# High parts of a square copied in SBUF, and subtractions issued a step later, in an attention-and-channel-mix kernel

## The chip, the cores and the metric

The kernel runs on one core of one Trainium2 chip. Five engines work beside each other, each from a queue of its own and in that queue's order: TensorE (PE, with its weight loads shown as PEld) multiplies matrices into PSUM, VectorE (DVE) and ScalarE (ACT) work on PSUM and SBUF, GpSimd (POOL) works on SBUF, and SyncE (SP) issues DMAs. The metric is the device time of one execution in microseconds.

## The reference

Four batches of 12,608 tokens of 128 channels go through an attention over 32 inducing points and then through a channel mix:

```python
h = mab(I, x)
return mab(x, h).astype(np.float32)          # attn_out, B x N x 128
...
xk = mu_k * x + (1.0 - mu_k) * x_prev
xr = mu_r * x + (1.0 - mu_r) * x_prev
k = np.maximum(xk @ w_k, 0.0)
v = k * k @ w_v
r = 1.0 / (1.0 + np.exp(-(xr @ w_r)))
return (r * v).astype(np.float32)
```

`mab(q, kv)` is softmax attention with kv as keys and values; `x_prev` is `x` moved by one token. The hidden width of the channel mix is 1,024.

## The kernel before

The channel mix is cut into groups of 512 tokens (25 in a batch, the last of 320) and each group into four units of two chunks of the hidden width: 400 units, numbered `n`. For one unit, `up` (L800) multiplies into a PSUM buffer `ps_a`, of which there are two; `square` (L803 to L819) makes the squared ReLU; `down` (L829) multiplies it with `w_v` into `ps_v`. The products run on operands of type fp32r, so that a factor is split in two: a high part `kh`, rounded to fp32r, and a low part `kl`, which is the square less `kh`. `down` takes three products: high with high, high with the low weights, and low with high.

In `square`, VectorE takes the ReLU from PSUM into `k` (L810). The high part is then the square of `k` on ScalarE (L815), or, for the units in the set `high_vector`, the product of the ReLU of `ps_a` and `k` on VectorE (L812), which reads PSUM once more. ScalarE squares `k` in place (L816), and GpSimd subtracts, `kl = k - kh` (L818). `k` has four buffers, `kh` five and `kl` four.

The order of all instructions is written out by hand in the loop at L1011. In step `n` it issues, if `n` is even, the up products of units `n` and `n + 1`; then the work listed in `early`; then `square` of unit `n` with its subtraction; then the gate product `zgate` (once in a group), `store`, `down` of unit `n - 4`, and last what is listed in `events` for this step. `gate` (L834) of a finished group stands at the head of a step.

`events` holds the preparation of what comes later. While the units of one batch run, in stretches of twelve steps, each of six stretches has `stage_a` of the following batch (its scores against the inducing points, L340 to L452) and `stage_b` (the second attention of the next block of the same batch, L617 to L663, with DMAs that lay out its results as `R`). `combine` closes the sum of a batch at its end. The last batch has no following one, so that its stretches hold only `stage_b`. `high_vector` is filled in the same loop (L993): with `s` the first step of a stretch, units `s + 4` and `s + 8`, 48 in all; each batch has some 28 units behind its six stretches in which none is on VectorE.

At the start, `head` and `start` run the first batch's attention and the conversion of the weights. Their last parts stand in `events` of steps 0 and 1: `place(3)` in step 0 holds L115, the conversion L109 on GpSimd and L110 on ScalarE, and L120; `place` in step 1 holds L123, L127, L133 on GpSimd, and `split_wv` with L162 on ScalarE and L163 on GpSimd. Aside from these and its share of the weights before, GpSimd's queue holds nothing but the 400 subtractions.

Of the kernel before, what the change touches and what calls it, by code (L numbers as in the profile page):

```python
# [8 lines left out]
F32 = mybir.dt.float32  # L9
# [4 lines left out]
ALU = mybir.AluOpType  # L14
# [5 lines left out]
def kernel(  # L20
# [11 lines left out]
    nc = tc.nc  # L32
# [741 lines left out]
    class Group:  # L774
# [28 lines left out]
        def square(self, u, on_vector):  # L803

            w = self.w
            k = mp.tile([P, UC * G], F32, name="k_t", bufs=4).rearrange("p (c t) -> p c t", c=UC)[:, :, :w]
            kh = mp.tile([P, UC, G], F32R, name="kh", bufs=5)[:, :, :w]
            kl = mp.tile([P, UC, G], F32R, name="kl", bufs=4)[:, :, :w]
            ps = self.ps.pop(u)[:, :, :w]
            nc.vector.tensor_scalar(out=k, in0=ps, scalar1=0.0, scalar2=None, op0=ALU.max)  # L810
            if on_vector:
                nc.vector.scalar_tensor_tensor(out=kh, in0=ps, scalar=0.0, in1=k,  # L812
                                               op0=ALU.max, op1=ALU.mult)
            else:
                nc.scalar.activation(out=kh, in_=k, func=AF.Square)  # L815
            nc.scalar.activation(out=k, in_=k, func=AF.Square)  # L816
            self.h[u] = (kh, kl)
            return lambda eng, a, z: eng.tensor_tensor(out=kl[:, :, a:z], in0=k[:, :, a:z],  # L818
                                                       in1=kh.bitcast(F32)[:, :, a:z], op=ALU.subtract)  # L819

        def down(self, u):
            w = self.w
# [33 lines left out]
    def run(th):  # L856
        for f in th:
            f()
# [51 lines left out]
    def head():  # L910


        last = NBLK - 1
        for k in range(2):
            ab[k].tr()
        ab[0].scores()
        for k in range(NBLK):
            ab[k].maxi()
            ab[k].expo()
            if k > 0:  # L920
                ab[k - 1].hmm()
                ab[k - 1].acc()
            if k == last:
                maxes()
            if k == 0:
                constants()
            if k + 2 < NBLK:
                ab[k + 2].tr()
            place(PARTS[k][1])
            if k == last:  # L930
                ab[k].sums()
                weights()
            ab[k].etrans()
            ab[k].ecopy()
            if k < last:
                ab[k].sums()
                ab[k + 1].scores()
        weights_sum()
        place(2)
        ab[last].hmm()  # L940
        ab[last].acc()
        load_x(1, 0)
        place(1)
        hfin()
        place(1)
# [11 lines left out]
    def start():  # L957

        def bank():
            return pv.tile([P, G], F32, name="ps_v")  # L960

        wk = wpart(0, bank)
        wg = wpart(1, bank)
        sc0, df0, ex0, nm0, hi0, lo0, turn0, put0, idle = stage_b_first(0)
        sc1, df1, ex1, nm1, hi1, lo1, turn1, put1, _ = stage_b_first(1)
        run([sc0, wk[0], sc1, df0, ex0, nm0, wk[1], hi0, wk[2], lambda: idle(2), lambda: turn0(0), lambda: put0(0),
             lo0, lambda: turn0(1), lambda: put0(1)])
        run([df1, ex1])
        at(0, lambda: place(3))
        at(1, lambda: place(len(work)))  # L970
        at(0, wg[0])
        (b_scores, b_trans, b_maxi, b_sub, b_expo, b_total, b_recip, b_mult, b_back, b_high, b_low,
         b_spread) = stage_b(0, 0, None, 0, "a")
        for f in (nm1, hi1):
            soon(1, f)
        for n, fs in ((0, (b_scores,)), (2, (b_trans, b_maxi, b_sub, b_expo)),
                      (3, (b_total, b_recip, b_mult, b_back, b_high)), (4, (b_low,))):
            for f in fs:
                at(n, f)
        for i in range(2, Q):  # L980
            at(i + 3, lambda i=i: b_spread(i))
            at(i + 5, lambda i=i: double(batches[0], i))
        for n, f in ((1, lo1), (1, wg[1]), (1, wg[2]), (2, lambda: turn1(0)), (2, lambda: turn1(1)),
                     (2, lambda: put1(0)), (2, lambda: put1(1)), (2, lambda: units[0][0].zgate())):
            at(n, f)

    SEG = 12
    high_vector = set()
    for b in range(B):
        t = b * UB + (4 if b == 0 else 0)  # L990
        for j in range(NBLK - 1):
            s = t + SEG * j
            high_vector |= {s + 4, s + 8}  # L993
            if b + 1 < B:
                stage_a(b + 1, j, at, s)
            stage_b(b, j + 1, at, (s - 2 if j == (b == 0) else s + 1) if b or j else 4, direct=b == j == 0)
        if b + 1 < B:
            s = t + SEG * (NBLK - 1)
            combine(b + 1, at, s)
            stage_b(b + 1, 0, at, s + 10)  # L1000
    units = []
    for b in range(B):
        for g in range(NG):
            grp = Group(b, g)
            units += [(grp, u) for u in range(NU)]
    end = len(units) - 1
    late = []
    with tc.manual_schedule():
        head()
        start()  # L1010
        for n in range(len(units) + LAG + 2):  # L1011
            grp, u = units[n] if n < len(units) else (None, n % NU)
            old, ou = units[n - LAG] if LAG <= n < len(units) + LAG else (None, 0)
            m = n - LAG - 1
            if 0 <= m < len(units) and units[m][1] == NU - 1:
                units[m][0].gate()
            if grp is None:
                run(late)
                late = []
            else:  # L1020
                if n % 2 == 0:
                    for g, v in units[n:n + 2]:
                        g.up(v)
                run(early.pop(n, []))
                low = grp.square(u, n in high_vector)
                run(late)
                late = []
                part = grp.w - (grp.w // 2 if n >= len(units) - 3 else 0)
                low(nc.gpsimd, 0, part)
                if part < grp.w:  # L1030
                    late = [lambda low=low, a=part, z=grp.w: low(nc.vector, a, z)]
                if n == end:
                    run(late)
                    late = []
                if n >= NU and u == 1:
                    grp.zgate()
            if 1 <= m <= len(units) and units[m - 1][1] == NU - 1:
                units[m - 1][0].store()
            if old is not None:
                old.down(ou)  # L1040
            run(events.pop(n, []))
# [30 lines left out]
```

## Time and profile before

| what | us |
|---|---|
| median of 3 runs | 1134.17 |
| lowest and highest | 1133.51, 1136.06 |
| the profiled execution | 1133.0 |
| its span, first to last instruction | 1131.1 |
| TensorE busy | 1074.4 |
| VectorE busy | 912.4 |
| ScalarE busy | 963.7 |
| GpSimd busy | 955.0 |

The page's shares (95%, 81%, 85% and 84% of the span in the order of the table) are averages. Matmuls are pipelined and their busy time counts waits within the pipeline, so that a TensorE that is busy throughout need not be at its peak. The mean granted TensorE clock was 0.978 of full speed; it was below 0.9 only in the first 113 us. In the profile, a row of a group gives line, engine, operation, target and sources, shapes, count, then busy time and mean nanoseconds of one, then the idle time of the engine ahead of it and what ended it. A row of the timeline gives start and length in microseconds, and in square brackets the idle time ahead and what ended it.

### The profile page before, as it was taken

What the parts mean: (1) busy time and instruction counts of PE and PEld (TensorE: products, weight loads), DVE (VectorE), ACT (ScalarE), POOL (GpSimd) and SP (SyncE); (2) the same over time, 40 slices, a digit from 0 to 9 for tenths busy, and PEclk for the clock granted to TensorE, in tenths of its full rate; (3) what the DMA queues carried; (4) which work ended last, traced back from release to release, by engine and by line L of the source; (5) the groups of instructions that cost most, each with busy time, mean ns of one, the idle gap of its engine ahead of it and who ended that gap; (6) DMA issues with size and microseconds to landing.
All of it is one profiled execution on the core that took longest, in us unless ns stands there. A gap on an engine that the chain in (4) does not pass through costs nothing.

```text
span 1131.1 us, 19193 instructions
## 1 busy us (share of the span) xinstructions
PE 1074.4 (95%) x6530; PEld 735.9 (65%) x6530; DVE 912.4 (81%) x1289; ACT 963.7 (85%) x1103; POOL 955.0 (84%) x422
## 2 busy tenths in 40 slices
PE   7647999999999999999999999999999999999996
PEld 5424666666766666666767666666667666667775
DVE  3666889998787899998677899998777788888665
ACT  5356788998898989899998989989899989999994
POOL 1245788889888998889889898889889889999996
PEclk9768999999999999999999999999999999999999
DMA  9204476677216746766416656766424425443422
GB/s 265 82 3 110 94 156 143 159 165 167 50 28 139 166 115 150 171 146 142 85 25 127 144 123 154 159 134 146 79 44 94 76 50 105 85 94 75 88 37 34
DMA packets 268209, 124.64 MB, mean 110 GB/s; under 512 B 225904, under 2 KB 247440, under 8 KB 265808
## 3 DMA queue, kind: packets, MB, share of 16 engines
q1 hardware_dynamic: 267776, 123.40, 51.0%
q8 instruction: 52, 0.85, 0.3%
q14 instruction: 45, 0.37, 0.1%
q10 hardware_dynamic: 336, 0.02, 0.0%
HBM read 28.07 MB, written 25.82 MB: 48 GB/s over the span
## 4 chain that ended last, share of the span: by engine, by line
PE 77%; DVE 6%; POOL 5%; issue 4%; SPq 3%; ACT 3%; DMA 2%; DVEq 0%; ACTq 0%; POOLq 0%
PE ps_v L829 44%; PE ps_a L800 24%; POOL kl L818 4%; PE ps_v L788 3%; DVE k_t L810 2%; PE pb_b L617 2%; PE pb_a L368 2%; PE pb_a L437 1%; SPq L343 1%; SPq L192 1%; DMA kl<-in_x_dram 1%; ACT k_t L816 1%; ACT kh L815 1%; DMA R<-hl 1%; SPq L597 1%
## 5 line engine op out<-in xcount | busy, mean ns | idle before, releaser
L818 POOL TENSOR_TENSOR kl<-k_t,kh 128x1024 fp32r<-128x1024 f32 (+2 forms) x400 | 936.1, 2372 | 128.4 <-ACT k_t L816 103.3
L810 DVE TENSOR_SCALAR k_t<-ps_a 128x1024 f32<-128x1024 f32 (+1 forms) x400 | 477.2, 1198 | 94.6 <-PE ps_a L800 67.8
L816 ACT ACTIVATE k_t<-k_t 128x1024 f32<-128x1024 f32 (+1 forms) x400 | 417.8, 1047 | 51.7 <-DVE kh L812 18.9
L815 ACT ACTIVATE kh<-k_t 128x1024 fp32r<-128x1024 f32 (+1 forms) x352 | 365.1, 1037 | 63.7 <-DVE k_t L810 62.5
L800 PE MATMUL ps_a<-R,W 64*128 64x512 f32 (+1 forms) x2400 | 333.9, 408 | 18.1 <-DVE k_t L810 7.0
L800 PEld LDWEIGHTS ps_a<-R,W 64*128 64x128 f32 x2400 | 210.5, 186 | 140.4 <-issue 57.1
L829 PE MATMUL ps_v<-kh,wvh 128*128 128x512 f32 (+1 forms) x800 | 271.7, 421 | 0.0
L829 PE MATMUL ps_v<-kl,wvh 128*128 128x512 f32 (+1 forms) x800 | 247.3, 390 | 2.2 <-POOL kl L818 1.2
L829 PE MATMUL ps_v<-kh,wvl 128*128 128x512 f32 (+1 forms) x800 | 246.6, 390 | 0.0
L829 PEld LDWEIGHTS ps_v<-kh,wvh 128*128 128x128 f32 x800 | 132.8, 189 | 94.6 <-issue 35.1
L829 PEld LDWEIGHTS ps_v<-kl,wvh 128*128 128x128 f32 x800 | 149.7, 188 | 35.5 <-POOL kl L818 2.7
L829 PEld LDWEIGHTS ps_v<-kh,wvl 128*128 128x128 f32 x800 | 149.7, 188 | 33.4
L834 DVE TENSOR_TENSOR oT<-ps_v,rT 128x512 f32<-128x512 f32 (+1 forms) x100 | 66.9, 669 | 22.7 <-PE ps_v L829 22.0
L845 DVE STREAM_TRANSPOSE ot<-oT 128x512 f32<-128x512 f32 x96 | 67.0, 698 | 0.0
L788 PE MATMUL ps_v<-R,Wg 128*128 128x512 f32 (+1 forms) x200 | 63.1, 397 | 0.6 <-DVE oT L834 0.5
L812 DVE SCALAR_TENSOR_TENSOR kh<-ps_a,k_t 128x1024 fp32r<-128x1024 f32 x48 | 58.8, 1225 | 1.7
L790 ACT ACTIVATE rT<-ps_v 128x512 f32<-128x512 f32 (+1 forms) x100 | 57.8, 578 | 0.3
L340 DVE STREAM_TRANSPOSE xs<-xb 128x512 f32<-128x512 f32 x72 | 49.9, 694 | 3.6 <-DMA R<-hl 1.9
L788 PEld LDWEIGHTS ps_v<-R,Wg 128*128 128x128 f32 x200 | 36.6, 189 | 11.5 <-DVE oT L834 3.0
L790 ACT ACT_TABLE_LOAD x31 | 39.8, 1283 | 0.5
L663 DVE TENSOR_TENSOR hl<-pb_b,hl 128x512 fp32r<-128x512 f32 x23 | 15.8, 689 | 14.8 <-ACT hl L660 14.5
L617 PE MATMUL pb_b<-xt,hT 128*32 128x512 f32 x184 | 24.4, 603 | 0.0
(212 smaller groups left out, 538.4 us busy)
## 6 DMA issues: line engine op xcount, KB each, us to landing
out_dram<-ot SPq DMA_DIRECT2D x184, 128.0 KB, 3.3
R<-R SPq DMA_DIRECT2D x90, 256.0 KB, 3.3
xb<-in_x_dram SPq DMA_DIRECT2D x18, 1024.0 KB, 5.9
xt<-xs SPq DMA_DIRECT2D x288, 64.0 KB, 2.0
R<-hl SPq DMA_DIRECT2D x98, 128.0 KB, 2.4
R<-hl SPq DMA_DIRECT2D x98, 127.8 KB, 2.4
kh<-in_x_dram SPq DMA_DIRECT2D x4, 512.0 KB, 8.2
kl<-in_x_dram SPq DMA_DIRECT2D x4, 512.0 KB, 7.6
```

Of the source, the lines that this page charges most:

```text
L340: nc.vector.transpose(out=xs.rearrange("p (s q) -> p s q", q=M), in_=S.xb[j][:, :, M * c:M * (c + 1)])
L788: nc.tensor.matmul(out=ps[:, :w], lhsT=S.Wg, rhs=R[:, s, :w], start=(s == 0), stop=(s == 1))
L790: nc.scalar.activation(out=self.rT, in_=ps[:, :w], func=AF.Sigmoid)
L800: nc.tensor.matmul(out=ps[:, r, :w], lhsT=S.W[a][rows, u * P:(u + 1) * P], rhs=R[rows, k, :w], start=(n == 0), stop=(n == 2))
L810: nc.vector.tensor_scalar(out=k, in0=ps, scalar1=0.0, scalar2=None, op0=ALU.max)
L812: nc.vector.scalar_tensor_tensor(out=kh, in0=ps, scalar=0.0, in1=k, op0=ALU.max, op1=ALU.mult)
L815: nc.scalar.activation(out=kh, in_=k, func=AF.Square)
L816: nc.scalar.activation(out=k, in_=k, func=AF.Square)
L818: return lambda eng, a, z: eng.tensor_tensor(out=kl[:, :, a:z], in0=k[:, :, a:z], in1=kh.bitcast(F32)[:, :, a:z], op=ALU.subtract)
L829: nc.tensor.matmul(out=self.v, lhsT=wt[:, fc, :], rhs=kk[:, c, :], start=(fc == 0 and n == 0), stop=(fc == FC - 1 and n == 2))
L834: nc.vector.tensor_tensor(out=self.oT, in0=self.v, in1=self.rT, op=ALU.mult)
L845: nc.vector.transpose(out=ot[:, o:o + w], in_=self.oT)
```

## The change

`square` now returns two functions. `high` copies the finished square `k` from SBUF into `kh` on VectorE, for the units of `high_vector`; for these units ScalarE does only the square in place. `low` is the subtraction on GpSimd. Both are issued in the following step, behind that step's `square`; only the last four units keep them in their own step, with the tail's halves as before. Four units in twelve are in `high_vector` in place of two.

```diff
-            if on_vector:
-                nc.vector.scalar_tensor_tensor(out=kh, in0=ps, scalar=0.0, in1=k,
-                                               op0=ALU.max, op1=ALU.mult)
-            else:
+            if not on_vector:
                 nc.scalar.activation(out=kh, in_=k, func=AF.Square)
             nc.scalar.activation(out=k, in_=k, func=AF.Square)
             self.h[u] = (kh, kl)
-            return lambda eng, a, z: eng.tensor_tensor(out=kl[:, :, a:z], in0=k[:, :, a:z],
-                                                       in1=kh.bitcast(F32)[:, :, a:z], op=ALU.subtract)
+
+            def low(eng, a, z):
+                eng.tensor_tensor(out=kl[:, :, a:z], in0=k[:, :, a:z],
+                                  in1=kh.bitcast(F32)[:, :, a:z], op=ALU.subtract)
+
+            def high():
+                if on_vector:
+                    nc.vector.tensor_copy(out=kh, in_=k)
+            return high, low
...
-            high_vector |= {s + 4, s + 8}
+            high_vector |= {s + 1, s + 4, s + 8, s + 10}
...
-                low = grp.square(u, n in high_vector)
-                run(late)
-                late = []
+                high, low = grp.square(u, n in high_vector)
+                run(late + after)
+                late, after = [], []
                 part = grp.w - (grp.w // 2 if n >= len(units) - 3 else 0)
-                low(nc.gpsimd, 0, part)
+                if n < len(units) - 4:
+                    after = [high, lambda low=low, z=grp.w: low(nc.gpsimd, 0, z)]
+                else:
+                    high()
+                    low(nc.gpsimd, 0, part)
```

More of the change, by code (lines that the diff above doesn't have):

```diff
@@ L1024 @@
                 run(early.pop(n, []))
-                low = grp.square(u, n in high_vector)
-                run(late)
-                late = []
+                high, low = grp.square(u, n in high_vector)
+                run(late + after)
+                late, after = [], []
                 part = grp.w - (grp.w // 2 if n >= len(units) - 3 else 0)
-                low(nc.gpsimd, 0, part)
+                if n < len(units) - 4:
[3 more added lines that the diff above has]
+                    low(nc.gpsimd, 0, part)
                 if part < grp.w:
```

## The prediction

> **What bounds the kernel now.** I read the windows view first, cut into stretches of twelve units, because the page's shares average over stages with different limits. Its columns are the length of the stretch, then busy microseconds (and instructions) of each engine.
>
> ```profile
> core 0: us, PE busy (x) PEld busy (x) DVE busy (x) ACT busy (x) POOL busy (x), PEclk, DMA share, GB/s
> ...
> 686.98:718.88 31.90, 31.90 (x201) 21.53 (x199) 29.84 (x43) 28.66 (x33) 28.71 (x13) 1.00 0.63 142
> ...
> 916.71:946.35 29.64, 29.64 (x160) 20.61 (x158) 25.13 (x30) 27.11 (x29) 26.39 (x12) 1.00 0.42 80
> 946.35:976.00 29.65, 29.65 (x161) 20.62 (x159) 25.14 (x30) 27.54 (x31) 28.48 (x13) 1.00 0.44 81
> 976.00:1005.64 29.64, 29.64 (x160) 20.61 (x158) 25.12 (x30) 27.35 (x30) 28.43 (x13) 1.00 0.41 81
> 1005.64:1034.60 28.96, 28.96 (x160) 20.62 (x159) 24.38 (x30) 26.76 (x29) 27.77 (x13) 1.00 0.45 84
> 1034.60:1063.24 28.64, 28.64 (x153) 20.47 (x151) 22.00 (x27) 27.21 (x31) 28.64 (x13) 1.00 0.42 82
> ```
>
> In the middle of a batch (first row) TensorE is never idle and sets the 31.90 us; VectorE is left 2.06 us and GpSimd 3.19 us. In the last batch no following batch is prepared, TensorE has less to do, and the stretch falls to 29.65 and then 28.64 us, where GpSimd is busy throughout: twelve subtractions are then the bound. Next I read the page's groups for the edited lines.
>
> ```profile
> L818 POOL TENSOR_TENSOR kl<-k_t,kh 128x1024 fp32r<-128x1024 f32 (+2 forms) x400 | 936.1, 2372 | 128.4 <-ACT k_t L816 103.3
> ...
> L815 ACT ACTIVATE kh<-k_t 128x1024 fp32r<-128x1024 f32 (+1 forms) x352 | 365.1, 1037 | 63.7 <-DVE k_t L810 62.5
> ...
> L845 DVE STREAM_TRANSPOSE ot<-oT 128x512 f32<-128x512 f32 x96 | 67.0, 698 | 0.0
> ...
> L812 DVE SCALAR_TENSOR_TENSOR kh<-ps_a,k_t 128x1024 fp32r<-128x1024 f32 x48 | 58.8, 1225 | 1.7
> ```
>
> **What the edits remove and add.** High parts on VectorE go from 2 to 4 in twelve, 48 to 96. ScalarE loses 48 squares of 1.037 us, 49.8 us over the run, 2.07 us a stretch. That is worth little by itself: in the middle TensorE is full, and ScalarE was not its limit. VectorE loses 2 x 1.225 us a stretch and gains four copies.
>
> No copy from SBUF to SBUF of this size is in the trace. The nearest row is a one-input operation between SBUF tiles, 512 elements wide.
>
> ```profile
> L115 DVE TENSOR_SCALAR xs<-k_t x4: 415/420/421, 20.9 to 62.7; 128x512 int32<-128x512 int32 x4
> ```
>
> It took 0.420 us, where the transpose of 512 elements (L845) took 0.698. The 0.278 us between them is what 256 elements cost L845, 1.09 ns each, so L115 handled elements two at a time. 1,024 elements in pairs should take what 512 take singly, **0.69 us**. The other end is singly, 1.22 us, as L812. I take 0.69, since L115 is the same kind of operation; open is whether an fp32r target keeps the pace. The Trainium skill, VectorE: DVE Perf Modes, section The perf-mode tier table, gives fp32 copies in SBUF twice the pace of operations with two inputs; the L115 row agrees for int32, and no row shows it for fp32r.
>
> VectorE per middle stretch: 29.84 - 2.45 + 4 x 0.69 = 30.15 of 31.90 us, if no copy has to wait. But there are rows that say it will.
>
> ```profile
> 310.77 2.41 POOL L818 TENSOR_TENSOR kl<-k_t,kh 128x1024 fp32r<-128x1024 f32 x1 [1.61 <-ACT k_t L816]
> ...
> 312.29 0.93 DVE L524 TENSOR_SCALAR mk<-stack,rd 128x32 f32<-128x32 f32 x1
> ```
>
> ```profile
> 65.01 2.37 POOL L818 TENSOR_TENSOR kl<-k_t,kh 128x1024 fp32r<-128x1024 f32 x1 [11.78 <-ACT k_t L816]
> ```
>
> ```profile
> 65.71 2.21 DVE L123 SCALAR_TENSOR_TENSOR e1t<-k_t,e1t 128x512 f32<-128x512 uint32 x1
> ```
>
> ```profile
> L123 DVE SCALAR_TENSOR_TENSOR e1t<-k_t,e1t x4: 681/688/2210, 25.7 to 65.7; 128x512 f32<-128x512 uint32 x4
> ```
>
> ```profile
> 1114.24 5.58 POOL L818 TENSOR_TENSOR kl<-k_t,kh 128x1024 fp32r<-128x1024 f32 x4
> ```
>
> ```profile
> 1115.30 4.87 DVE L818 TENSOR_TENSOR kl<-k_t,kh 128x320 fp32r<-128x320 f32 x1
> ```
>
> L524, a one-input operation of 32 elements from SBUF, began inside a GpSimd subtraction and ended at 313.22, just behind that subtraction's end (313.18). L123 (median 0.688 us) took 2.21 us and ended 0.54 us behind GpSimd's end at 67.38. The narrow L818 on VectorE started at 1115.30 and ended at 1120.17, 0.35 us behind the last of four subtractions in a row (1119.82). So these VectorE operations wait for GpSimd, and the third got no turn between two subtractions. The Trainium skill, SBUF — State Buffer, section Who interferes with whom, has this as an exclusive lock on a port pair, held for a whole instruction, and counts copies in pairs under it. These three rows agree with the blocking; by a page without that rule the copies would cost nothing beyond 30.15 us, which is the second rival below.
>
> ```profile
> 63.88 1.06 ACT L816 ACTIVATE k_t<-k_t 128x1024 f32<-128x1024 f32 x1
> ```
>
> ```profile
> 697.85 9.53 POOL L818 TENSOR_TENSOR kl<-k_t,kh 128x1024 fp32r<-128x1024 f32 x4 [1.61 <-PE ps_a L800]
> ```
>
> What a copy then does: it stands in VectorE's queue behind the next unit's ReLU, and behind it stand that step's other VectorE work and the following ReLU, for which TensorE waits. The subtraction of the same unit waits for the copy, and the copy waits for the subtraction before it. So GpSimd stands still once per copied unit, at least 0.55 us (L123's rest for 512 elements) plus 0.07 us to start again (65.01, behind ScalarE's end at 64.94) and 0.03 us of lost overlap (a subtraction of 2.41 us follows the last by 9.53 / 4 = 2.38): with rounding, **0.66 us**, 0.80 (0.69 + 0.11) if the copy shares nothing with the wait, more if VectorE comes late.
>
> **Last batch.** Four copies cost GpSimd 4 x 0.66 = 2.6 us on twelve subtractions of 2.38 (28.5 us): 31.1 us. Against 29.64, 29.65, 29.64, 28.96 and 28.64 that is 1.5 x 3 + 2.1 + 2.5 = **+9** us. At 0.80 it is +12; if TensorE's lead on the entering side absorbs part, +5.
>
> **Middle stretches.** GpSimd at 31.1 of 31.90 still fits, so the price is what VectorE's waiting does to TensorE.
>
> ```profile
> 684.40 1.22 DVE L810 TENSOR_SCALAR k_t<-ps_a 128x1024 f32<-128x1024 f32 x1
> ```
>
> ```profile
> 685.38 1.67 PE L800 MATMUL ps_a<-R,W 64*128 64x512 f32 x12
> ```
>
> ```profile
> 700.13 1.22 DVE L810 TENSOR_SCALAR k_t<-ps_a 128x1024 f32<-128x1024 f32 x1
> ```
>
> The ReLU that ends at 685.62 frees the PSUM buffer for the second half of the up product of 685.38 (from 686.2, half of 1.67 us later): 0.6 us to spare. The copy of unit s+1 now comes ahead of it, 0.69 us, so 0.1 us is missing with no wait at all. Behind the ReLU of 700.13, which ends at 701.35, stands the copy of s+8; GpSimd's row of four from 697.85 gives it a turn at 702.6 (two of 2.38), so VectorE stands 1.3 us and copies until 703.2. L812 of the same unit, 1.23 us, is gone ahead of it, but the copies of s+4 and s+10 wait likewise. VectorE has 1.75 us a stretch to spare and four copies with waits of some 0 to 1.3 us: about 2.6 us, an overdraft of **0.8 us** a stretch (0 to 2.4, when each waits a whole 1.04 us). Twelve full stretches (four in each of three batches) at 0.8 and three lighter ones at 0.3: **+10.5** us (0 to 30).
>
> **Batch changes.** The chain of waits runs through the edited lines there.
>
> ```profile
> 617.39 1.07 ACT kh L815
> ...
> 624.81 1.23 DVE kh L812
> ...
> 626.18 0.98 PE ps_a L800 x6
> ```
>
> The square at 617.39 belongs to s+1, now a copy; and L812 no longer reads PSUM, so the up product follows the ReLU. 2.3 us leave the chain; the copy of s+1 gives about half back. Three changes at 1 us: **-3** us (0 to -7).
>
> **The start.** Subtractions are the only moved step that passes anything: on GpSimd's queue the first now stands behind the conversion L109, and the second behind L133 and L163; no DMA is issued in it, and no queue of SP is passed.
>
> ```profile
> 67.46 2.24 POOL L109 TENSOR_SCALAR s<-s 128x512 int32<-128x512 int32 x1
> 73.00 2.34 POOL L818 TENSOR_TENSOR kl<-k_t,kh 128x1024 fp32r<-128x1024 f32 x1 [3.30 <-ACT k_t L816]
> 75.30 1.26 POOL L133 TENSOR_TENSOR ot<-e1t,s 128x512 f32<-128x512 f32 x1
> ```
>
> ```profile
> 69.74 0.63 ACT L110 ACTIVATE s<-s 128x512 int32<-128x512 int32 x1 [4.28 <-POOL s L109]
> ```
>
> ```profile
> 53.26 0.43 DVE L105 TENSOR_SCALAR s<-k_t 128x512 int32<-128x512 int32 x1 [0.44 <-POOL ot L133]
> ...
> 54.54 0.42 DVE L723 TENSOR_TENSOR e<-e,mx 128x256 f32<-128x256 f32 x1
> ```
>
> ```profile
> 77.41 0.29 DVE L560 TENSOR_TENSOR Wg<-ps_v,Wg 64x128 fp32r<-64x128 f32 x1 [5.72 <-ACT Wg L556]
> ```
>
> L109 only needs L105 (done 53.69), but stood behind the subtraction of 65.01. It can now run at 53.8 to 56.0. ScalarE's 4.28 us wait at L110 goes; L133 comes behind the first subtraction and L127 at about 68.7 instead of 75.30, and what hung on it, L560 and then the third ReLU, 6.5 us earlier. What is late next: L723 has two SBUF inputs and falls into L109's new place, up to 1.2 us late, with the first ReLU behind it. Net **-5.5** us (-6.5 to 0, if something else of the start is late).
>
> **Sum.** The execution profiled took 1133.0 us (span 1131.1, 1.9 around it): 1133.0 + 9 + 10.5 - 3 - 5.5 = 1144. The median shown is 1.2 us above that execution: **1145**.
>
> **The rivals.** (1) *The waits are covered, faster.* If a copy usually meets GpSimd idle (it has 3.19 us idle in the middle), or is let in between two subtractions, the middle costs nothing and the last batch 0 to 5: 1134 - 8.5 + 0 to 5, some **1127**. For it: L524 did come through at the next boundary. Against it: the last batch has no idle time to give. It decides if GpSimd's pause per copy is under about 0.3 us. (2) *One element at a time, no lock.* VectorE needs 29.84 - 2.45 + 4.88 = 32.27 of 31.90: +0.4 in twelve stretches, 4.5 in all, less 8.5: **1130**. For it: the fp32r target is unseen. Against it: L115. (3) *No turn until GpSimd's row ends*, as in 1115.30, where the wait was 4.4 us. If two copies in a stretch wait one subtraction more (2.37 us), the overdraft grows by about 3 us with ReLUs late in turn: 15 x 3 + 12 + 0.8 x 12 - 8.5, some **1190**.
>
> **Chances.** Forecast 0.52 (1136 to 1158), rival 1 0.22, rival 2 0.12, rival 3 0.14. A measurement of this kernel can tell about 0.2% (2.3 us) from no change. Faster beyond it: 0.20 + 0.06; within it: 0.02 + 0.05 + 0.04; slower: 0.48 + 0.01 + 0.14. The range 1126 to 1166 holds the forecast, most of rivals 1 and 2 and the lower part of rival 3; outside lie about 0.1 below and 0.1 above.
>
> **What would show it.** Copy rows of a median well over 0.69 us whose ends lie 0.55 us behind a subtraction's end show the lock; rows of 1.2 us that ignore GpSimd show rival 2. The start is right if the third ReLU begins near 72 instead of 77.73. The last batch is right if its stretches are about 31 us; the middle, if 31.90 becomes about 32.7 with TensorE waiting for L810's successor. The forecast is wrong if the middle stays at 31.90 and the last batch under 30.

## The result, and the profile after

The changed kernel takes 1166.28 us (median of 4 runs, 1164.24 to 1167.71) against 1133.84 us before in the same comparison: a ratio of 1.0282, with a 95% interval of 1.0260 to 1.0304. It is slower by 32 us; 1145 had been forecast, with a range of 1126 to 1166. The direction was right, the size a third of what came.

The page's groups after the change come first (line, engine, operation, tiles, count, busy time, mean nanoseconds, idle time ahead and what ended it). The subtraction now has the line L817, the squares L812 and L813, the copy L822.

```profile
L817 POOL TENSOR_TENSOR kl<-k_t,kh 128x1024 fp32r<-128x1024 f32 (+2 forms) x400 | 936.9, 2371 | 160.9 <-DVE kh L822 71.5
...
L822 DVE CAST kh<-k_t 128x1024 fp32r<-128x1024 f32 x96 | 140.4, 1463 | 35.9 <-ACT k_t L813 34.9
```

A copy takes 1.463 us on average, not 0.69, and VectorE stood idle for another 35.9 us ahead of the copies, nearly all of it for ScalarE's square. The view of that line alone gives the least, the median and the greatest length:

```profile
L822 DVE CAST kh<-k_t x96: 682/1332/2921, 83.7 to 1085.8; 128x1024 fp32r<-128x1024 f32 x96
```

The least, 0.682 us, is the price without a wait. Next the windows view over the same stretches of twelve units as before, the first in the middle of a batch, the second in the last batch:

```profile
core 0: us, PE busy (x) PEld busy (x) DVE busy (x) ACT busy (x) POOL busy (x), PEclk, DMA share, GB/s
701.49:735.27 33.78, 32.91 (x200) 21.23 (x199) 31.79 (x45) 26.53 (x31) 28.63 (x13) 1.00 0.61 135
...
970.31:1002.93 32.62, 30.60 (x160) 20.39 (x159) 30.10 (x32) 25.80 (x28) 28.56 (x13) 1.00 0.42 77
```

The stretches grew from 31.90 to 33.78 and from 29.65 to 32.62 us. TensorE, which had been busy throughout both, now stands still within them. ScalarE has more than 6 us a stretch to spare, and the kernel gains nothing from it in these stretches.

Where the 33.5 us of span came from is read from the trace by the start of `down`'s first product of some units. The parts add up to the spans (1164.59 and 1131.12).

| from the product of unit ... to that of unit ... | before, us | after, us | difference |
|---|---|---|---|
| start of the span to 12 | 128.77 | 123.97 | -4.8 |
| 12 to 100 (first batch) | 231.12 | 238.51 | +7.4 |
| 100 to 200 | 261.90 | 271.37 | +9.5 |
| 200 to 300 | 261.34 | 270.86 | +9.5 |
| 300 to the end of the span (last batch) | 247.99 | 259.88 | +11.9 |

### The profile page after: what moved, and what is told of

The parts are those of the page before. It is cut to its first block, busy times and chain, and to the rows that moved or that the text cites. A ratio compares the mean times of both kernels' runs of the same rounds, so it can differ in the third digit from the quotient of the medians.

```text
span 1164.6 us, 19063 instructions
## 1 busy us (share of the span) xinstructions
PE 1092.2 (94%) x6530; PEld 730.4 (63%) x6530; DVE 978.9 (84%) x1337; ACT 914.9 (79%) x1055; POOL 955.9 (82%) x422
## 4 chain that ended last, share of the span: by engine, by line
PE 49%; DVE 22%; ACT 7%; issue 7%; SPq 5%; DMA 5%; POOL 4%; DVEq 0%; ACTq 0%; POOLq 0%
PE ps_v L833 26%; PE ps_a L800 15%; DVE k_t L810 10%; DVE kh L822 4%; POOL kl L817 3%; PE ps_v L788 3%; ACT kh L812 2%; ACT k_t L813 2%; SPq L343 2%; DVE ot L849 2%; DMA R<-hl 1%; DMA xt<-xs 1%; DVE oT L838 1%; DMA R<-R 1%; PE pb_a L437 1%
## 5 line engine op out<-in xcount | busy, mean ns | idle before, releaser
L817 POOL TENSOR_TENSOR kl<-k_t,kh 128x1024 fp32r<-128x1024 f32 (+2 forms) x400 | 936.9, 2371 | 160.9 <-DVE kh L822 71.5
L813 ACT ACTIVATE k_t<-k_t 128x1024 f32<-128x1024 f32 (+1 forms) x400 | 413.7, 1046 | 75.0 <-DVE k_t L810 46.0
L812 ACT ACTIVATE kh<-k_t 128x1024 fp32r<-128x1024 f32 (+1 forms) x304 | 315.1, 1036 | 131.0 <-DVE k_t L810 130.8
L800 PE MATMUL ps_a<-R,W 64*128 64x512 f32 (+1 forms) x2400 | 346.3, 413 | 35.6 <-DVE k_t L810 24.9
L800 PEld LDWEIGHTS ps_a<-R,W 64*128 64x128 f32 x2400 | 207.0, 186 | 173.9 <-DVE k_t L810 68.6
L822 DVE CAST kh<-k_t 128x1024 fp32r<-128x1024 f32 x96 | 140.4, 1463 | 35.9 <-ACT k_t L813 34.9
L788 PEld LDWEIGHTS ps_v<-R,Wg 128*128 128x128 f32 x200 | 35.9, 192 | 19.5 <-DVE oT L838 12.1
```

The lines of the kernel that those rows point to most:

```text
L788: nc.tensor.matmul(out=ps[:, :w], lhsT=S.Wg, rhs=R[:, s, :w], start=(s == 0), stop=(s == 1))
L800: nc.tensor.matmul(out=ps[:, r, :w], lhsT=S.W[a][rows, u * P:(u + 1) * P], rhs=R[rows, k, :w], start=(n == 0), stop=(n == 2))
L817: eng.tensor_tensor(out=kl[:, :, a:z], in0=k[:, :, a:z], in1=kh.bitcast(F32)[:, :, a:z], op=ALU.subtract)
L822: nc.vector.tensor_copy(out=kh, in_=k)
```

## What the trace shows at the copies

Four rows of VectorE and GpSimd in the middle stretch (start, length, in brackets the idle time ahead and what ended it):

```profile
706.11 0.69 DVE L822 CAST kh<-k_t 128x1024 fp32r<-128x1024 f32 x1 [1.51 <-ACT k_t L813]
...
715.89 2.22 DVE L822 CAST kh<-k_t 128x1024 fp32r<-128x1024 f32 x1
...
712.78 4.78 POOL L817 TENSOR_TENSOR kl<-k_t,kh 128x1024 fp32r<-128x1024 f32 x2 [1.08 <-ACT k_t L813]
718.25 2.41 POOL L817 TENSOR_TENSOR kl<-k_t,kh 128x1024 fp32r<-128x1024 f32 x1 [0.69 <-DVE kh L822]
```

The second copy lasts 2.22 us and ends at 718.11, 0.55 us behind the end of GpSimd's row of two at 717.56; then GpSimd, which paused 0.69 us, goes on. That is the wait which the prediction read from the trace before, and its price is close to the foreseen one (0.55 and 0.66 us). Of the 96 copies 73 last over 0.8 us, and each of them ends 0.55 to 0.56 us behind a subtraction's end. The Trainium skill, SBUF — State Buffer, section Who interferes with whom, says that a copy in a two-port mode and a GpSimd instruction exclude each other for an instruction's whole length; this trace agrees.

The first copy waits for nothing of GpSimd. VectorE stands 1.51 us idle ahead of it for the square of its own unit. ScalarE's rows say why that square is late:

```profile
702.87 1.28 ACT L404 ACT_TABLE_LOAD   x1
704.16 0.29 ACT L404 ACTIVATE alpha<-mkr,nb 128x1 f32<-128x1 f32 x1
704.37 0.67 ACT L405 ACTIVATE e1t<-pb_a,nb 128x512 f32<-128x512 f32 x1
704.94 0.19 ACT L405 ACTIVATION_READ_ACCUMULATOR e1t<-pb_a,nb 128x1 f32 x1
705.03 1.05 ACT L813 ACTIVATE k_t<-k_t 128x1024 f32<-128x1024 f32 x1
```

The exponentials of the batch after and their table load, 2.2 us, stand ahead of the square in ScalarE's queue. In the kernel before, VectorE waited for a square only once, 1.3 us in the tail. The same stretch of that kernel already shows what was coming:

```profile
687.94 1.28 ACT L404 ACT_TABLE_LOAD   x1
...
690.10 1.05 ACT L816 ACTIVATE k_t<-k_t 128x1024 f32<-128x1024 f32 x1
```

```profile
688.57 1.23 DVE L812 SCALAR_TENSOR_TENSOR kh<-ps_a,k_t 128x1024 fp32r<-128x1024 f32 x1
689.71 1.21 DVE L810 TENSOR_SCALAR k_t<-ps_a 128x1024 f32<-128x1024 f32 x1
```

The ReLU behind which the copy was to stand ended at 690.92 and the square at 691.15, 0.2 us later. The edit takes the L812 of 1.23 us from ahead of that ReLU, so that VectorE arrives that much sooner and would wait about 1.4 us; it waits 1.51.

In the middle stretch the four copies (units s+1, s+4, s+8, s+10) wait 0.41, 1.51, 1.53 and 0.12 us, 3.6 us together; the second of these waits is on ScalarE, the others are on GpSimd. The prediction had left VectorE 1.75 us for waits. 3.6 - 1.75 is 1.8, and the stretch grew by 1.9. So its account by overdraft comes out here once the waits are 3.6 us where it put 2.6. That it comes out so closely is in part luck: by the stretch's own row VectorE was busy for 31.79 us, waits within the copies included, and 1.51 us ahead of one copy make 33.3, not 33.8. In every experiment below with four high parts in twelve such a sum, or 31.90 where that is more, falls 0.3 us or more short of the stretch.

In the last batch VectorE has time in plenty, but its order does the same harm:

```profile
980.50 2.34 DVE L810 TENSOR_SCALAR k_t<-ps_a 128x1024 f32<-128x1024 f32 x2
983.92 2.32 DVE L822 CAST kh<-k_t 128x1024 fp32r<-128x1024 f32 x1 [1.08 <-ACT k_t L813]
986.17 0.70 DVE L849 STREAM_TRANSPOSE ot<-oT 128x512 f32<-128x512 f32 x1
986.80 1.18 DVE L810 TENSOR_SCALAR k_t<-ps_a 128x1024 f32<-128x1024 f32 x1
```

Between the ReLU that ends at 982.84 and the next one at 986.80 VectorE stands for ScalarE (1.08) and for GpSimd (1.63 of the 2.32), copies and transposes. The waits view of that last-batch stretch (who waited for whom, us in total, times, longest) shows the price on TensorE, as weight loads and as products:

```profile
PEld ps_a L800 <- DVE k_t L810: 3.3, 3, 1.6
...
PE ps_a L800 <- DVE k_t L810: 1.9, 2, 1.1
```

TensorE's products stand 1.9 us in the stretch until ReLUs free a PSUM buffer, nearly all of the 2.0 us in which they stand at all; the weight loads' 3.3 us are the same stops, seen from the loads ahead of the products, and do not add to them. In the stretch of before one weight load waited, and no product did:

```profile
PEld ps_a L800 <- DVE k_t L810: 0.4, 1, 0.4
```

## The experiments

Two theories stood at first. A: VectorE's waits at the copy, for GpSimd and for ScalarE, make the ReLUs behind it late. B: GpSimd's pause at each copied unit is the cost by itself. A third, C, was the mere number of high parts on VectorE. All ratios are to the kernel before as measured beside each (its medians there were 1133.8 to 1134.9 us). Edits are shown against the changed kernel, in extracts. The stretches named "middle" and "last" are units 224 to 236 and 324 to 336.

| kernel | us | ratio (95%) | middle | last |
|---|---|---|---|---|
| before | 1133.84 | | 31.90 | 29.65 |
| changed | 1166.28 | 1.0282 (1.0260 to 1.0304) | 33.78 | 32.62 |
| order only | 1127.30 | 0.9935 (0.9922 to 0.9948) | 31.90 | 29.65 |
| four products from PSUM | 1148.35 | 1.0121 (1.0105 to 1.0136) | 33.27 | 29.76 |
| copy through PSUM | 1176.01 | 1.0362 (1.0345 to 1.0379) | 35.05 | 31.65 |
| copy two steps later | 1135.22 | 1.0008 (0.9998 to 1.0019) | 32.39 | 31.27 |
| mixed | 1119.54 | 0.9859 (0.9843 to 0.9875) | 32.13 | 29.65 |
| copy of the ReLU | 1149.50 | 1.0126 (1.0105 to 1.0147) | 33.45 | 30.20 |
| copy, one element at a time | 1154.83 | 1.0168 (1.0150 to 1.0185) | 33.83 | 30.61 |
| copy at the end of the step | 1138.87 | 1.0042 (1.0025 to 1.0058) | 32.20 | 31.42 |
| two steps later, no copy | 1125.55 | 0.9925 (0.9904 to 0.9946) | 31.90 | 29.65 |

### Order only

```diff
-            high_vector |= {s + 1, s + 4, s + 8, s + 10}
+            high_vector |= {s + 4, s + 8}
...
-            if not on_vector:
+            if on_vector:
+                nc.vector.scalar_tensor_tensor(out=kh, in0=ps, scalar=0.0, in1=k,
+                                               op0=ALU.max, op1=ALU.mult)
+            else:
                 nc.scalar.activation(out=kh, in_=k, func=AF.Square)
...
-                    nc.vector.tensor_copy(out=kh, in_=k)
+                    pass
```

> Only the subtractions go a step later; two high parts in twelve, as the product from PSUM, as in the kernel before. If the changed kernel's early part (first finished product of unit 12 at 123.97 us against 128.77) comes from GpSimd's order at the start alone: about 5 us less than before, 1129 us, and middle stretches at 31.90 and last-batch stretches at 29.65 as before. If the step's move itself costs something in the middle: 1134 or more, with stretches over 32.

It took 1127.3 us, less than the kernel before, and its later stretches are those of before. The unit-12 mark came at 123.52. So the subtractions' new place is a gain made wholly at the start, and beside this kernel four copies in place of two products cost 39 us rather than 32. GpSimd's rows of the changed kernel show how the start gains:

```profile
52.21 1.92 POOL L109 TENSOR_SCALAR s<-s 128x512 int32<-128x512 int32 x1 [0.55 <-DVE s L105]
63.12 2.38 POOL L817 TENSOR_TENSOR kl<-k_t,kh 128x1024 fp32r<-128x1024 f32 x1 [8.99 <-ACT k_t L813]
66.73 1.64 POOL L133 TENSOR_TENSOR ot<-e1t,s 128x512 f32<-128x512 f32 x1 [1.23 <-DVE s L127]
```

The conversion L109 runs at 52.21 instead of 67.46, behind no subtraction, and L133 at 66.73 instead of 75.30. Where the order alone was changed they run at 52.91 and 67.29.

### Four products from PSUM

```diff
-            if not on_vector:
+            if on_vector:
+                nc.vector.scalar_tensor_tensor(out=kh, in0=ps, scalar=0.0, in1=k,
+                                               op0=ALU.max, op1=ALU.mult)
+            else:
                 nc.scalar.activation(out=kh, in_=k, func=AF.Square)
...
-                    nc.vector.tensor_copy(out=kh, in_=k)
+                    pass
```

> Four high parts in twelve, but each as the product that reads PSUM, and issued in its own step; subtractions a step later. No wait on GpSimd and none on ScalarE stands ahead of it. Theory A (VectorE's waits at the copy delay the ReLUs): VectorE has 29.84 + 2.45 = 32.3 us of work for 31.90, so middle stretches near 32.4 and last-batch stretches at 29.65; about 1129 + 12 x 0.5 = 1135. Theory C (it is the number of high parts on VectorE, not their kind): middle near 33.8, last batch near 32.6, 1160 or more.

```profile
697.63:730.90 33.27, 32.73 (x201) 21.24 (x199) 32.19 (x45) 26.76 (x31) 28.65 (x13) 1.00 0.61 136
```

In the last batch four products cost next to nothing (29.76), which speaks against theory C there. In the middle they cost 1.4 us, more than the 0.5 expected from a sum of VectorE's work: VectorE is busy for 32.2 of 33.3 us, and over the run TensorE's products waited 5.6 us for these operations, which still read the buffer. The total of 1148 lies between the two expectations. As these operations are longer than a copy and hold PSUM, the run does not say what the number alone costs in the middle; the runs below, with as many copies at 32.20 and 32.39, leave it 0.5 us of the 1.9 at most.

### Copy through PSUM

```diff
-                    nc.vector.tensor_copy(out=kh, in_=k)
+                    nc.vector.scalar_tensor_tensor(out=kh, in0=z, scalar=0.0, in1=k,
+                                                   op0=ALU.mult, op1=ALU.add)
```

Here `z` is the PSUM buffer of the following unit, whose ReLU was just taken.

> The copy of the changed kernel in the same place, but as 0 x (PSUM of the next unit) + square, so with one SBUF input and one element at a time. Its wait on ScalarE's square stays, its wait on GpSimd should go: durations of 1.22 to 1.24 us throughout. Theory A: VectorE has 29.84 - 2.45 + 4.9 = 32.3 us of work and 1.5 us of waits for ScalarE for 31.90, so middle stretches of 32.5 to 33.8; the last batch, where VectorE has time, falls from 32.6 to between 29.65 and 30.5; total 1140 to 1155. Theory B (GpSimd's pause at each copied unit is the cost): the last batch stays at 31 or more, since each subtraction still waits for its copy.

The copies are even at 1.2 us, so the wait on GpSimd is gone, but the kernel is slower still, far above the 1140 to 1155 expected. Its line view names the reason: the copy now holds a buffer that TensorE wants.

```profile
L822 DVE SCALAR_TENSOR_TENSOR kh<-ps_a,k_t x96: 1199/1214/1226, 84.4 to 1095.9; 128x1024 fp32r<-128x1024 f32 x96
...
  POOL kl L817: 84.0, 67
  PEld ps_a L800: 48.7, 42
  PE ps_a L800: 32.0, 34
```

The last rows count who waited for this line: TensorE's weight loads 48.7 us, and its products 32.0 us of the same stops. That cost is the experiment's own, so the run decides nothing between A and B.

### Copy two steps later

```diff
-                late, after = [], []
+                late, after, soon_after = [], soon_after, []
...
-                    after = [high, lambda low=low, z=grp.w: low(nc.gpsimd, 0, z)]
+                    soon_after = [high, lambda low=low, z=grp.w: low(nc.gpsimd, 0, z)]
...
```

> Copy and subtraction two steps later in place of one. ScalarE's square is then long finished when the copy's turn comes, so VectorE's idle time ahead of the copies (35.9 us) should fall below 5 us; the wait on GpSimd stays possible. Theory A: the middle stretch falls from 33.76 by about the 1.5 us of that wait, to 32.2, unless the waits on GpSimd grow by as much; total 1140 to 1150. Theory B: GpSimd pauses as before, 1160 to 1170.

With the same 96 copies and the same exclusion, 31 of the 32 us are gone, a little more than theory A expected. VectorE no longer idles ahead of a copy, and the copies are shorter (mean wait inside a copy 0.44 us instead of 0.77). Theory B as the whole cost falls. The subtractions' place is not what freed the stretches: without copies the two stretches take 31.90 and 29.65 us with the subtractions one step later as well as two (order only; two steps later, no copy). It does give 3.4 of the 31 us, at the start (the unit-12 mark is at 120.52).

The copies are not free here either: without them the same order takes 1125.55 us, 9.7 us less. There B has its place: the last-batch stretch stays at 31.27, and every copied unit there has a pause of 0.7 us on GpSimd.

```profile
680.78:713.17 32.39, 32.28 (x201) 21.36 (x199) 31.19 (x45) 26.78 (x31) 28.55 (x13) 1.00 0.64 142
940.72:971.99 31.27, 30.12 (x161) 20.38 (x159) 28.55 (x33) 25.70 (x28) 28.54 (x12) 1.00 0.39 70
```

28.54 us of subtractions and 4 x 0.69 of pauses make 31.3: the account that the prediction gave for the last batch (31.1), seen alone.

### Copy of the ReLU

```diff
-            nc.scalar.activation(out=k, in_=k, func=AF.Square)
+            q = mp.tile([P, UC, G], F32, name="q_t", bufs=1)[:, :, :w] if on_vector else k
+            nc.scalar.activation(out=q, in_=k, func=AF.Square)
...
-                eng.tensor_tensor(out=kl[:, :, a:z], in0=k[:, :, a:z],
+                eng.tensor_tensor(out=kl[:, :, a:z], in0=q[:, :, a:z],
```

> The changed kernel, but the copies take the ReLU and not its square, and for these units the square goes to a tile of its own (one buffer): the copy has no wait on ScalarE left, while its wait on GpSimd and its place in VectorE's queue stay. The high part of those units is then that of the ReLU. If ScalarE's wait is what overdraws VectorE in the middle (1.5 of 3.6 us of waits a stretch, 1.75 us to spare): 33.76 falls to between 32.3 and 32.9; last batch 32.6 falls by at most 1. If only the wait on GpSimd counts, it grows by what ScalarE's shrinks, and the stretches stay at 33.8 and 32.6.

The low part of these units is then the square less the ReLU and no longer small, and `down` leaves out its product with the low weights, so that the result is not the reference's; the run stands for its times alone.

The last batch fell by 2.4 us, more than expected, the middle by only 0.3. In the last batch the copy now comes early enough to stand between two subtractions that are both ready:

```profile
940.08 1.75 DVE L823 CAST kh<-k_t 128x1024 fp32r<-128x1024 f32 x1
```

```profile
941.24 2.86 POOL L818 TENSOR_TENSOR kl<-k_t,kh 128x1024 fp32r<-128x1024 f32 x1
```

The copy ends at 941.83, 0.55 us behind the subtraction before (938.86 to 941.28); the following subtraction is already begun and lasts 2.86 instead of 2.41 us. So a copy between two ready subtractions costs GpSimd 0.45 us, against a pause of 0.69 where the subtraction must wait for it. Over the run 25 copies came in this way, and the subtraction then running lasted 2.84 to 2.91 us. For the middle the reading is clouded: ScalarE waited 43.7 us over the run for the one buffer `q_t`, so what VectorE's wait for the square alone is worth there stays open.

### Copy, one element at a time

```diff
-                    nc.vector.tensor_copy(out=kh, in_=k)
+                    nc.vector.tensor_scalar(out=kh, in0=k, scalar1=0.0, scalar2=None, op0=ALU.max, op1=ALU.add,
+                                            accum_out=sm.tile([P, 1], F32, name="sink", bufs=2))
```

> The changed kernel, but the copy is max(square, 0) with a running sum written out beside it, in the same place: one element at a time, one SBUF input. If such an operation does not wait for GpSimd, its durations are even, 1.2 to 1.4 us. Then, if waiting for GpSimd is what costs the last batch its time (VectorE has over 4 us to spare there): from 32.6 to between 29.65 and 30.6. If the pause of GpSimd or the place behind the ReLU alone is the cost: 31 or more. The middle, where VectorE has 33.1 us of work for 31.90: 33.1 to 34.7.

This form does not wait for GpSimd:

```profile
L822 DVE TENSOR_SCALAR_CACHE_REDUCE kh<-k_t x96: 1190/1210/1221, 85.0 to 1075.7; 128x1024 fp32r<-128x1024 f32 x96
...
968.13:998.74 30.61, 30.19 (x161) 20.60 (x159) 26.96 (x36) 25.77 (x28) 28.55 (x13) 1.00 0.43 82
```

All 96 take 1.2 us, and the last batch falls from 32.62 to 30.61, though each operation itself is longer. Together with the run before: taking away either wait, on ScalarE or on GpSimd, takes 2.0 to 2.4 of the 3.0 us from a last-batch stretch. At the copy of 983.92 they follow one another, and the first makes the second long: while VectorE waits for the square, GpSimd begins its next subtraction, which VectorE must then sit out. The middle stayed at 33.8, since VectorE got back 2.1 us of waiting and was given about as much work (31.84 us busy in the stretch, without waits, for 31.79 with them).

### Copy at the end of the step

```diff
-                run(late + after)
-                late, after = [], []
+                run(late)
+                late = []
...
             run(events.pop(n, []))
+            run(after)
+            after, again = again, []
...
```

> The changed kernel, but copy and subtraction stand at the end of the following step, behind its other VectorE work, and not right behind its ReLU; they still stand ahead of the ReLU after that. ScalarE's square is then done in most cases. If the waits at the copy are the cost, middle stretches fall to between 32.2 and 33 and the last batch, where little other work stands ahead of the copy, stays within 1 us of 32.6; about 1150. If the place ahead of the next ReLU is what counts, whatever the wait: 1160 or more.

```profile
682.48:714.68 32.20, 32.20 (x201) 21.35 (x199) 30.41 (x45) 26.54 (x31) 28.62 (x13) 1.00 0.64 142
```

The copies stand behind the step's other VectorE work but still ahead of the next ReLU, and the middle is 32.20: with the waits down to about 0.7 us a stretch, the place ahead of a ReLU costs little. The total of 1139 is below the 1150 expected, and the last batch fell by 1.2 us, a little more than expected; it keeps the pauses of GpSimd (31.42).

### Mixed, and two steps later without copies

From the stretch times a faster version could be put together: subtractions two steps later, copies only in the first stretch of a batch, two products from PSUM in all other stretches.

```diff
-            high_vector |= {s + 1, s + 4, s + 8, s + 10}
+            high_copy |= {s + 1, s + 4, s + 8, s + 10} if j == 0 else set()
+            high_vector |= {s + 4, s + 8} if j else set()
...
```

> Subtractions two steps later throughout. In the first stretch of each batch four copies in twelve, as in the run with copies two steps later; in all other stretches two in twelve as the product from PSUM. If the stretch times of the earlier runs add up: first unit-12 mark at 120.5 us as in that run, 231.4 to the end of the first batch, 262.0 - 1.5 and 261.4 - 1.5 for the next two, 248.0 - 3.9 for the last: a span of 1116.5, a time of 1118. If the gains at the batch changes hang on copies in the later stretches too, or if subtractions two steps later cost something where the product from PSUM is used: 1124 or more.

It took 1119.54 us, 1.4% less than the kernel before. The last run took its copies away again (this edit is against the mixed kernel):

```diff
-            high_copy |= {s + 1, s + 4, s + 8, s + 10} if j == 0 else set()
-            high_vector |= {s + 4, s + 8} if j else set()
+            high_vector |= {s + 4, s + 8}
```

> As the mixed kernel, with subtractions two steps later throughout, but without copies: two in twelve as the product from PSUM in every stretch. If the mixed kernel's gain at the batch changes comes from its copies: the stretches of units 100 to 112 and 200 to 212 go back from 31.8 to 33.3, that of 300 to 312 from 29.7 to 33.6, together 6.9 us, and the time is about 1126. If it comes from the subtractions' place: 1120, as the mixed kernel.

It took 1125.55 us (1121.89 to 1129.53, a wider spread than the others; the fastest had a mean clock of 0.986, the slowest of 0.979). Between the two, the first stretch of the last batch shows what the copies are worth there, first with them, then without:

```profile
872.91:902.64 29.73, 29.73 (x161) 20.52 (x159) 25.90 (x29) 26.63 (x28) 27.65 (x13) 1.00 0.48 95
```

```profile
875.01:907.07 32.06, 30.29 (x161) 20.50 (x159) 25.46 (x31) 28.72 (x31) 28.52 (x13) 1.00 0.45 89
```

With the copies TensorE is never idle. The three batch changes differ by 1.5, 1.8 and 2.3 us, 5.6 together where 6.9 had been expected; the medians differ by 6.0, and the spans of the two profiled executions by 4.6, since the mixed kernel is 0.9 us behind by unit 100. So copies are worth their price at the batch changes, and not elsewhere. That it is ScalarE's part of the chain there which they shorten was not tested alone.

## Why the prediction was right and wrong

- **The bounds** (TensorE in the middle, GpSimd behind it in the last batch) were right: a kernel with nothing else changed keeps 31.90 and 29.65, and relief for ScalarE gave nothing there.
- **The copy at 0.69 us** was right; the least of the 96 is 0.682, and an fp32r target keeps the pace.
- **The exclusion of copy and subtraction** was right, in place and price: ends 0.55 us behind a subtraction, pauses of 0.69 us for 0.66.
- **The start, -5.5 us,** was right in its mechanism: L109 and L133 moved forward as foreseen. The -4.8 us of the changed kernel and the -4.9 of span of the order alone come closer to it than the rows bear out. L105, ahead of all that moved, began at 51.70 in the changed kernel's profile and at 53.26 in that of before, so 1.6 of the 4.8 us are not shown to be the edit's. Counted from L105 the third ReLU came 6.6 us earlier (6.5 foreseen), of which 3.2 were left at unit 12. One detail was wrong: L723 was not held up by L109 in its new place (below).

```profile
51.70 0.43 DVE L105 TENSOR_SCALAR s<-k_t 128x512 int32<-128x512 int32 x1 [0.44 <-POOL ot L133]
...
69.55 1.22 DVE L810 TENSOR_SCALAR k_t<-ps_a 128x1024 f32<-128x1024 f32 x1
```

- **The batch changes, -3 us,** did not come: these stretches went by +0.8, +0.7 and -0.6 us. With copies two steps later they go by -1.5, -1.5 and -3.9, so a gain is there to be had; that the copies' waits took it back in the changed kernel fits the rows but was not tested alone. The last of the three is not all the copies': TensorE's granted clock there was 0.95 before, with 0.50 between 890.3 and 893.5 us (so the first 113 us were not the only ones below 0.9), and 1.00 in the runs that gained, of which the one without copies took 32.06.

```profile
883.13:916.71 33.58, 31.80 (x161) 21.56 (x159) 25.57 (x31) 29.03 (x31) 29.98 (x14) 0.95 0.43 84
```

- **The last batch, +9 us,** was +11.9, or +12.5 without the batch change at its head. The term counted GpSimd's pauses, which the run two steps later shows alone at the forecast size. It left out that a waiting copy makes ReLUs late for TensorE even where VectorE has time to spare.
- **The middle, +10.5 us, is the step that failed.** It put the overdraft at 0.8 us a full stretch, with waits of some 0 to 1.3 us at each of four copies. From unit 12 to unit 300 the loss was 26.4 us, 24.9 without the two batch changes in it, and 1.7 to 1.9 us in each full stretch of the second and third batch. One wait was missing from the sum: the prediction priced the waits on GpSimd (2.1 us measured, for 2.6) and none on ScalarE's square (1.5 us measured, behind a table load and two exponentials). The rows of ScalarE's queue ahead of the square were there to be read before.
- **The account by overdraft is only roughly right.** It adds VectorE's work and waits and compares the sum with 31.90. Four products from PSUM gave 32.3 of work and no wait at the copy, and took 33.27; copies two steps later and at the end of the step gave less than 31.90 and took 32.39 and 32.20. A late ReLU seems to cost TensorE something before VectorE is full, and the prediction's sum had no term for that.
- **The rivals.** Rival 2 (one element at a time, no exclusion) is refuted by the lengths, and so are copies in pairs without exclusion, which the prediction names in passing as that rival but does not price. Rival 3 (no turn until GpSimd's row ends) is refuted by the copies of the ReLU, 25 of which got their turn behind the running subtraction with another ready. Rival 1 (waits covered) is refuted by the 73 copies of 96 that waited; even two steps later, where VectorE waits less, the copies still cost 9.7 us beside the same order without them.

What stays open: how the loss in the middle divides between the two waits, since the run that removed ScalarE's gave ScalarE a wait of its own, and the run that removed GpSimd's made the copy longer.

## What to carry to other kernels

An instruction that is moved to an in-order engine brings all its waits into that engine's queue: list what each of its inputs waits for, and the queue ahead of that, before its own duration is priced. A cheaper instruction that must wait can be put one step further back, where its inputs are surely ready; here that was worth some 27 us with the same work, beside 3.4 us at the start from the subtractions' place. Where an edit has two parts, time each alone: the reordering was a gain of 0.65% and the copies beside it hid it.

## What the runs showed of the hardware

A VectorE copy that waits behind GpSimd gets its turn when the running subtraction ends, even if another is ready; that next one then lasts 2.86 us in place of 2.41. The tail of the kernel before, where a VectorE subtraction sat out four of GpSimd's, differs from this, and no run here says why. It was so in ten of the eleven traces, with three or four sat out; in the run with the copy one element at a time it came in behind the second of three.

Not every overlap holds an operation up. L723 reads two SBUF tiles on VectorE and ran inside L109 on GpSimd (52.21 to 54.13) without any delay, in the changed kernel and in all nine experiments:

```profile
52.97 0.43 DVE L723 TENSOR_TENSOR e<-e,mx 128x256 f32<-128x256 f32 x1
```

It took 0.43 us, as before (0.42). L109 works on one input, 512 elements in 1.92 us, and L723's second input is a broadcast of 8 values; which of these frees it was not tried.

The same copy written with a running sum beside it took 1.19 to 1.22 us in all 96 places, beside a GpSimd that worked through most of every stretch.
